# Placing loads on aligned runs of an on-chip arena, and asking for long loads at a smaller lead: a decode kernel bound by its loads

## The chip, the cores and the metric

The kernel runs on one core of one Trainium2 chip. The metric is device time in microseconds (us), median of several executions. Most kernels were timed in five rounds next to the kernel before, on the same chip. The spans of profiles (2343.0 us and so on) are those of one profiled execution. In the profiles PE is the matmul engine and PEld its weight loads, DVE, ACT and POOL are the vector, scalar and GpSimd engines, SP issues the loads; SBUF is the on-chip memory, in 128 partitions.

## The reference

Two layers of the same shape are applied twice to eight sequences with one new token each (`B = 8`, `D = 640`): attention over a cache, then a small feed-forward block.

```python
x = x + A(layernorm(x), k_cache, v_cache, wq, wo)   # layer 0
x = x + B(layernorm(x), w1, w2)
x = x + A(layernorm(x), k_cache, v_cache, wq, wo)   # layer 1, the same cache again
x = x + B(layernorm(x), w1, w2)
# A: q = x @ wq, 32 heads of 128; scores over 4096 cached keys, softmax, weighted sum of values, @ wo
# k_cache, v_cache: [8, 32, 4096, 128] bf16
```

One pass over both caches is 537 MB, and both layers need it, 1074 MB in all; the weights are 15 MB. There is one query per head, so there is little to compute per byte.

## The kernel before

All keys and values pass through one SBUF tile, the arena, of `G = 26` units. A unit is 4 KB in each of 128 partitions, 512 KB; one load is one DMA of `n` neighbouring units, from one run of memory to one run of the arena. For each batch entry layer 0 reads all its units in order; then comes the turn, and layer 1 reads them again. At the turn 21 units stay in the arena (`G - SPARE`) and three more are set aside, so that layer 1 need not load those 24 again. Over eight entries 1856 units are loaded out of 2048 read. While the 21 are kept, only five units are free, and loads are of one unit each.

A planner in Python decides, before anything runs, when each load is issued, how long it is and where it goes. It keeps a rough clock of the PE and of the loads; `lead` is how far the loads are planned to be ahead.

```python
G = 26
SPARE = 5
LEADS = ((9, 8), (6, 4), (5, 2))      # (lead in us, units): with that lead, a load has at least that many units
...
    def room(n):                      # where n free neighbouring units are; the longest free ones first
        us = [u for u in range(G - n + 1) if not any(owner[u : u + n])]
        return min(us, key=lambda u: max(freed[u : u + n])) if us else None

    def feed():                       # called whenever a unit has been read for the last time
        while at[0] < len(stream):
            lead = clock[1] - clock[0]
            calm = (PACE * (nth[stream[at[0]]] - at[1]) - LATE - lead) / 1.2
            least = next((n for us, n in LEADS if lead >= us), 1)
            least = min(least, max(1, (G - len(kept) - 2) // 3))
            most = min(max(least, int(calm)), LEADS[0][1], max(1, (len(stream) - at[0]) // 2))
            least = min(least, most)
            ...
            u = next((u for n in range(n, least - 1, -1) if (u := room(n)) is not None), None)
            if u is None:
                return                # no run of `least` units is free: hold out, issue nothing now
            ...
            ops.append(("load", b, p, n, u))
...
    def do_load(b, p, n, u):
        nc.sync.dma_start(out=arena[:, u * GW : (u + n) * GW], in_=A_kv[b, :, p * GW : (p + n) * GW])
```

A large lead makes the planner wait until a long run is free, in place of filling a short one at once.

## Time and profile before

| | before |
|---|---|
| median | 2340.99 us (6 runs, 2339.02 to 2343.42) |
| profiled span | 2343.0 us |
| moved by DMA | 990.87 MB |
| PE busy | 60% |
| rate between turns, most slices | 430 to 434 GB/s |

These are lines of the page of the kernel before: the span; the granted PE clock, the DMA share (tenths) and the rate in 40 slices of 58.6 us; two of the DMA queues with packets, megabytes and share of the 16 engines; the chain of waits by engine, then the head of its list by line.

```profile
span 2343.0 us, 43024 instructions
...
PEclk9999999999999998555555555555555555555555
DMA  9999999999999999999999999999999999999997
GB/s 411 430 433 401 433 432 432 431 396 432 432 432 430 404 434 431 430 427 403 433 432 431 426 412 434 430 432 420 427 431 427 432 416 430 431 431 431 396 433 329
...
q1 hardware_dynamic: 76564, 988.12, 99.4%
q8 instruction: 146, 2.39, 0.4%
...
DMA 71%; PE 17%; ACT 6%; DVE 3%; issue 2%; SPq 0%; POOL 0%; ACTq 0%; DVEq 0%; POOLq 0%
DMA arena<-in_A_kv_dram 71%; PE o_ps L687 5%; PE s_ps L695 4%; PE s_ps L705 2%; ACT P_row L755 2%; ACT o_sb L795 1%; PE small_ps L655 1%; DVE mrow L713 1%; ACT P_sb L761 1%; PE small_ps L800 1%; ACT arena L634 1%; PE small_ps L768 1%; PE small_ps L825 1%; DVE hmx L732 0%; ACT nmax L753 0%
```

The rate line is the one to read first. It stands mostly at 430 to 434 GB/s and dips at ten places: the first slice, the last one, and eight places about 280 us apart (401, 396, 404, 403, 412, 420, 416, 396) that hold the eight turns. The DMA share stays at 9 tenths through the dips: the engines are seldom idle there, they are less effective. The clock line falls to half at slice 17 and the rate line does not notice, so PE's speed is not what bounds this kernel. The Trainium skill's page "DMA: Bandwidth & Descriptors" (Specifications) gives 435 GB/s as the ceiling of the way into SBUF; the trace agrees, with 434 as the best slice. At 432.5 GB/s, 991 MB take 2291 us (worked out), so about 52 us of the span are open to any change of the loads.

These are lines of the page's list of DMA issues: count, KB of one, median us from issue to landing.

```profile
arena<-in_A_kv_dram SPq DMA_DIRECT2D x124, 4096.0 KB, 23.1
arena<-in_A_kv_dram SPq DMA_DIRECT2D x98, 2048.0 KB, 22.7
arena<-in_A_kv_dram SPq DMA_DIRECT2D x218, 512.0 KB, 6.5
arena<-in_A_kv_dram SPq DMA_DIRECT2D x48, 1024.0 KB, 11.3
```

The issue-to-landing time of 23 us for a 4096 KB load, whose bytes take 9.7 us, shows that such a load waits behind others. A one-unit load takes 6.5 us: at a turn it mostly has four others ahead of it (read from the issue and landing times), each 1.25 us.

### The profile page before, as it was taken

Reading aid. Unit: us, or ns where it says so; the run is one execution under the profiler, and the core shown is the slowest. Engines: PE = TensorE matmul, PEld = TensorE weight load, DVE = VectorE, ACT = ScalarE, POOL = GpSimd, SP = SyncE. Lnnn points to the kernel's source line nnn. Section 1 sums busy time; section 2 is a strip of 40 time slices with the busy share of each in tenths; the row PEclk is TensorE's granted clock in tenths of the full one; section 3 lists DMA queues with packets and bytes.
Section 4 is the critical chain, followed back from the end, with each engine's and each line's share of the span. In section 5 each row is a group of like instructions: output and inputs, shape, how many; then the busy total and the mean of one; then the engine's idle time right before and its main releaser. Section 6 shows DMA issues by size and latency. Waiting matters only on the chain.

```text
span 2343.0 us, 43024 instructions
## 1 busy us (share of the span) xinstructions
PE 1398.6 (60%) x18748; PEld 591.4 (25%) x18748; DVE 496.7 (21%) x2022; ACT 426.3 (18%) x986; POOL 59.5 (3%) x296
## 2 busy tenths in 40 slices
PE   3547654576545764557545675556755567545766
PEld 1214211152111511125111241113411133111523
DVE  1113211131112211122111221112211122111312
ACT  1111211122111221112211121111211112111211
POOL 0000000000000000000000000000000000000000
PEclk9999999999999998555555555555555555555555
DMA  9999999999999999999999999999999999999997
GB/s 411 430 433 401 433 432 432 431 396 432 432 432 430 404 434 431 430 427 403 433 432 431 426 412 434 430 432 420 427 431 427 432 416 430 431 431 431 396 433 329
DMA packets 76753, 990.87 MB, mean 423 GB/s; under 512 B 8596, under 2 KB 8596, under 8 KB 36500
## 3 DMA queue, kind: packets, MB, share of 16 engines
q1 hardware_dynamic: 76564, 988.12, 99.4%
q8 instruction: 146, 2.39, 0.4%
q14 instruction: 43, 0.35, 0.0%
HBM read 988.08 MB, written 0.01 MB: 422 GB/s over the span
## 4 chain that ended last, share of the span: by engine, by line
DMA 71%; PE 17%; ACT 6%; DVE 3%; issue 2%; SPq 0%; POOL 0%; ACTq 0%; DVEq 0%; POOLq 0%
DMA arena<-in_A_kv_dram 71%; PE o_ps L687 5%; PE s_ps L695 4%; PE s_ps L705 2%; ACT P_row L755 2%; ACT o_sb L795 1%; PE small_ps L655 1%; DVE mrow L713 1%; ACT P_sb L761 1%; PE small_ps L800 1%; ACT arena L634 1%; PE small_ps L768 1%; PE small_ps L825 1%; DVE hmx L732 0%; ACT nmax L753 0%
## 5 line engine op out<-in xcount | busy, mean ns | idle before, releaser
L687 PE MATMUL o_ps<-arena,P_sb 128*4 128x512 bf16 x3952 | 584.3, 596 | 402.0 <-DMA arena<-in_A_kv_dram 401.0
L695 PE MATMUL s_ps<-arena,qz 128*4 128x512 bf16 x3040 | 410.3, 602 | 261.1 <-DMA arena<-in_A_kv_dram 249.5
L687 PEld LDWEIGHTS <-P_sb 128*4 128x4 bf16 x3952 | 107.4, 88 | 502.8 <-issue 491.7
L713 DVE TENSOR_REDUCE mrow<-s_ps 100x1 bf16<-100x512 f32 x190 | 131.8, 694 | 323.2 <-PE s_ps L695 323.2
L795 ACT CAST o_sb<-o_ps 100x512 bf16<-100x512 f32 x247 | 144.9, 587 | 289.3 <-PE o_ps L687 286.0
L753 ACT ACTIVATE nmax<-small_ps 100x1 f32<-100x1 f32 x106 | 18.1, 171 | 774.5 <-PE small_ps L742 774.5
L775 DVE CAST P_sb<-small_ps 128x64 bf16<-128x64 f32 x190 | 42.6, 224 | 523.1 <-PE small_ps L768 523.1
L695 PEld LDWEIGHTS <-qz 128*4 128x4 bf16 x3040 | 63.9, 85 | 313.7 <-issue 295.5
L705 PEld LDWEIGHTS <-arena 128*128 128x128 bf16 x4224 | 129.6, 104 | 40.8 <-DMA arena<-in_A_kv_dram 23.4
L705 PE MATMUL s_ps<-qo,arena 128*128 128x1 bf16 x3712 | 123.7, 165 | 17.2 <-ACT P_sb L761 7.6
L768 PE MATMUL small_ps<-few,P_row 100*128 100x16 bf16 x760 | 52.3, 179 | 92.1 <-ACT P_row L755 92.1
L753 ACT ACTIVATE nmax<-small_ps,q_scale 100x1 f32<-100x1 f32 x84 | 22.0, 261 | 398.7 <-PE small_ps L742 398.7
L787 DVE TENSOR_REDUCE lsum<-small_ps 128x2 f32<-128x64 f32 x240 | 53.9, 224 | 171.9 <-PE small_ps L781 171.9
L768 PEld LDWEIGHTS <-P_row 100*128 100x128 bf16 x760 | 35.0, 107 | 186.5 <-ACT P_row L755 178.2
L720 PE MATMUL small_ps<-few,mrow 100*1 100x16 bf16 x190 | 34.4, 181 | 67.6 <-DVE mrow L713 67.6
L755 ACT ACTIVATE P_row<-s_ps,nmax 100x512 bf16<-100x512 f32 x106 | 72.8, 687 | 3.4
L800 PEld LDWEIGHTS <-o_sb 100*128 100x128 bf16 x988 | 45.7, 106 | 107.2 <-ACT o_sb L795 73.8
L655 PE MATMUL small_ps<-xq,wq_sb 128*128 128x1 bf16 x1200 | 48.8, 165 | 38.9 <-DVE qo L812 33.5
L800 PE MATMUL small_ps<-few,o_sb 100*128 100x2 bf16 x988 | 65.1, 170 | 10.7 <-DVE lsum L787 2.2
L727 DVE TENSOR_REDUCE diag<-small_ps 1x2 bf16<-1x16 f32 x190 | 30.8, 162 | 186.9 <-PE small_ps L720 186.9
L720 PEld LDWEIGHTS <-mrow 100*1 100x1 bf16 x190 | 15.0, 79 | 210.8 <-DVE mrow L713 210.8
L755 ACT ACTIVATE P_row<-s_ps,nmax,q_scale 100x512 bf16<-100x512 f32 x84 | 65.3, 778 | 2.8
(225 smaller groups left out, 958.0 us busy)
## 6 DMA issues: line engine op xcount, KB each, us to landing
arena<-in_A_kv_dram SPq DMA_DIRECT2D x124, 4096.0 KB, 23.1
arena<-in_A_kv_dram SPq DMA_DIRECT2D x98, 2048.0 KB, 22.7
arena<-in_A_kv_dram SPq DMA_DIRECT2D x218, 512.0 KB, 6.5
arena<-in_A_kv_dram SPq DMA_DIRECT2D x48, 1024.0 KB, 11.3
arena<-in_A_kv_dram SPq DMA_DIRECT2D x11, 3072.0 KB, 22.4
arena<-in_A_kv_dram SPq DMA_DIRECT2D x11, 2560.0 KB, 20.5
arena<-in_A_kv_dram SPq DMA_DIRECT2D x10, 1536.0 KB, 19.7
wq_sb<-in_A_wq_dram SPq DMA_DIRECT2D x4, 1280.0 KB, 17.6
```

The lines of the kernel that those rows point to most:

```text
L655: nc.tensor.matmul(q_ps[:, h : h + 1], lhsT=wq_sb[:, g, c, (2 * n + h) * Dh : (2 * n + h + 1) * Dh], rhs=xlns[b][:, 0, c : c + 1], start=( ...
L687: nc.tensor.matmul(o_ps[32 * c : 32 * c + CJ, :], lhsT=P_tiles[i][:, h, j : j + CJ], rhs=arena[:, at + c * CJ * Dh : at + (c + 1) * CJ * D ...
L695: nc.tensor.matmul(s_ps[32 * c : 32 * c + CJ, :], lhsT=qz[:, i % 3, c // 2, 3 - g : 3 - g + CJ], rhs=arena[:, at + c * BANK : at + (c + 1) ...
L705: nc.tensor.matmul(s_tiles[i][:, j : j + 1], lhsT=arena[:, at + n * P : at + (n + 1) * P], rhs=qo[:, b, h : h + 1], start=True, stop=True,)
L713: nc.vector.tensor_reduce(out=m_tiles[i][:OR, :1], in_=s_ps[:OR], axis=AX.X, op=ALU.max)
L720: nc.tensor.matmul(turn_ps[:1, : 4 * CJ], lhsT=m[:OR, :1], rhs=rsel[:OR], start=True, stop=True)
L755: nc.scalar.activation(out=P_rows[i][:OR], in_=s_ps[:OR], func=ACT.Exp, bias=nm[:OR, :1], scale=more)
L768: nc.tensor.matmul(P_ps[:, k * 4 * CJ : (k + 1) * 4 * CJ], lhsT=P_row[:OR, k * P : (k + 1) * P], rhs=rsel[:OR], start=True, stop=True,)
L775: nc.vector.tensor_copy(out=P_tiles[i].rearrange("p h (c k) -> p h c k", k=BANK // P), in_=P_ps.rearrange("p (k h c) -> p h c k", k=BANK / ...
L787: nc.vector.tensor_reduce(out=L, in_=(lsum2_ps if ahead[i] else lsum_ps).rearrange("p (h j) -> p h j", h=2), axis=AX.X, op=ALU.add)
L795: nc.scalar.copy(out=o_tiles[i][:OR], in_=o_ps[:OR, :].rearrange("p (j d) -> p j d", j=CJ))
L800: nc.tensor.matmul(oy[i][:, :2], lhsT=o_tiles[i][:OR, j, :], rhs=gsel[:OR, j, :], start=(j == 0), stop=(j == CJ - 1))
```

## The change

The intent: free runs on an 8-unit boundary (4-unit for shorter loads) are taken first, and loads of one or two units go into blocks already in use, so that whole blocks stay free for long loads. And a long load needs less lead than it did: with 7 us under way a load must have eight units (it took 9 us), with 5 us four (6), with 4 us two (5).

```diff
-LEADS = ((9, 8), (6, 4), (5, 2))
+LEADS = ((7, 8), (5, 4), (4, 2))
...
     def room(n):
         us = [u for u in range(G - n + 1) if not any(owner[u : u + n])]
-        return min(us, key=lambda u: max(freed[u : u + n])) if us else None
+        step = 8 if n > 4 else 4 if n > 2 else n
+
+        def cost(u):
+            block = owner[u // 8 * 8 : u // 8 * 8 + 8]
+            return u % step, -sum(block) if n <= 2 else 0, max(freed[u : u + n])
+
+        return min(us, key=cost) if us else None
```

The bytes, the order in which units are loaded and all compute work are the same. Only lengths, places and times of issue of the loads move.

## The prediction

> **What bounds the kernel now.** The loads of keys and values. The page's DMA part has 988 MB on queue 1, 430 to 434 GB/s in most of the 40 slices; PE is busy 60% and the chain of waits lies 71% in arena loads. The Trainium skill ("DMA: Bandwidth & Descriptors", Specifications) gives a ceiling of 435 GB/s; the trace agrees. At 432.5 GB/s all 991 MB would take 2291 us (my division), so only some 52 us of the 2343 us span can be won. Stretches of 5 us show where: 3 us at the start, 13.6 at the end (the last 10.6 have no load under way), and some 29 at eight turns from layer 0 to layer 1 of a batch entry, near 205, 490, 785, 1070, 1360, 1640, 1920 and 2190 us, 2.3 to 4.4 us each.
>
> **What goes on at a turn.** 21 of the 26 arena units hold kept data; the other five take loads of one unit (512 KB), three or four under way, landing every 1.25 us where long loads take 1.2125 us per unit, plus one to three single delays of 0.5 to 1.4 us. These come while loads are queued: the trace shows 16 KB packets on the instruction queue, each some 0.9 us, every 6 us at a turn and every 25 us elsewhere. Between turns the queue holds some 13 us of work at each issue, so no wait of the issuing queue costs anything there.
>
> **What the change does.** Bytes and compute work stay. Loads that the changed program issues: one-unit 218 to 207, two-unit 48 to 38, four-unit 98 to 63, eight-unit 124 to 149; 521 loads become 484. Eight-unit loads off an 8-unit boundary fall from 32 to 9. The five spare units at a turn, and so its one-unit loads, stay.
>
> **Cost.** A packet of 4 KB takes 167 ns on the mean against 152 at the long ones' rate, 8 KB 311 against 304, 16 KB 616 against 608. Fewer of them save, as an estimate, 11 x 128 x 15 ns / 16 = 1.3 us, 0.5 us and 2.4 us: 4.2 us at most. By landing times four-unit loads are no slower per byte when the queue is full, so I count 0.5 to 2 us. Perhaps 1 to 2 us more come from the first turn, the worst (about 5 us), whose pattern becomes like the others'. Holding out for long runs at a thinner lead may cost 1 us when the queue refills after a turn. In sum 2 to 4 us of 2341.
>
> **Prediction.** 2338 us, 2329 to 2346 in 8 of 10. Faster by over 2%: 1%; within 2%: 98%; slower: 1%.
>
> **What would show it.** Right: DMA issues with the counts above; eight dips of GB/s, still 2 to 4.5 us each; between turns 10 us or more queued at each issue; the last landing still 10 to 11 us before the end; 146 instruction packets. Wrong: dips half as deep (then fragmented short loads caused them), or new dips 20 to 60 us after each turn with PE waiting for the arena (then holding out drains the queue).
>
> **What would make it wrong.** A longer load waits for more units and lands all at once; if PE at the 0.5 clock of the second part falls behind there, DMA would starve. Or alignment itself speeds transfers in a way that landing times of before don't show. The last loads (5, 1, 2, 1, 1 units instead of 7, 4, 2, 1, 1) could move the end by a microsecond or two.

## The result, and the profile after

| | before | after |
|---|---|---|
| median | 2340.99 us (6 runs) | 2343.64 us (6 runs, 2341.00 to 2345.82) |
| ratio after over before | | 1.0011, 95% interval 0.9998 to 1.0024 |
| loads | 521 | 484 |

A ratio here and below is the mean time of one kernel's fast runs over the mean of the other's fast runs of the same rounds, so it is not quite the ratio of the medians quoted beside it. By this ratio the change is the same within noise; if anything it is slower.

The same lines of the page after:

```profile
span 2344.0 us, 42943 instructions
...
PEclk9999999999655555555555555555555555555555
DMA  9999999999999999999999999999999999999997
GB/s 411 431 431 402 431 431 432 431 410 434 430 434 428 405 429 430 431 428 404 435 431 431 423 410 432 432 432 417 415 434 433 430 413 422 431 432 430 395 433 337
...
q1 hardware_dynamic: 71236, 988.12, 99.4%
q8 instruction: 146, 2.39, 0.4%
```

```profile
arena<-in_A_kv_dram SPq DMA_DIRECT2D x149, 4096.0 KB, 23.0
arena<-in_A_kv_dram SPq DMA_DIRECT2D x63, 2048.0 KB, 13.8
arena<-in_A_kv_dram SPq DMA_DIRECT2D x207, 512.0 KB, 6.4
arena<-in_A_kv_dram SPq DMA_DIRECT2D x38, 1024.0 KB, 9.5
```

The counts are those forecast: 149 long loads in place of 124, 63 of four units in place of 98. The rate between turns is mostly 430 to 434 GB/s as before, and the eight dips are there (402, 410, 405, 404, 410, 415, 413, 395). Instruction packets are 146 in both. This chain of waits breaks off (its shares add up to 28% of the span), so it is not used. The granted clock of the six runs of the changed kernel lies between 0.62 and 0.94, and a higher clock did not go with a shorter time (2344.78 us at 0.94, 2341.00 at 0.62).

To see where the two differ, the landing times of loads were read from the two traces and set against the position in the stream of 1856 units, which is the same for both. About a quarter of the loads (129 of 521 before, 119 of 484 after) have no landing time in the profile's own view and were bridged by a straight line. Three sums over the run, each the time taken less 1.2125 us per unit, the pace of long loads:

- turn: from four units ahead of the first one-unit load of a turn to its last, 26 to 30 units, eight times (the bounds are those of the kernel before, and the same stretches of the stream are used for every kernel);
- refill: the 60 units after that, in which layer 1 gives the kept units free and the queue grows back, eight times;
- rest: all else after the first 160 units.

```
profiled kernel          turn  refill  rest   (us, sums over the run)
before                   25.0    6.9    9.8
after                    23.9   10.2    8.8
```

The missing landings can be got back: the records are short only because the load of `x` and the store of the result leave 11 of them where the other transfers leave 16. With every landing read, no sum in this text moves by more than 1.5 us (the two refills become 6.2 and 9.6).

So the turns lose about what they lost, and the refill loses 3 us more. That is the size of the whole difference, but single delays of about 1.2 us fall differently in every execution, so one pair of profiles does not prove it. Here is a refill in both: windows of 20 us after the seventh turn (busy us and count of instructions by engine, then clock, DMA share and rate). First the kernel before, with the header line:

```profile
core 0: us, PE busy (x) PEld busy (x) DVE busy (x) ACT busy (x) POOL busy (x), PEclk, DMA share, GB/s
1940.00:1960.00 20.00, 15.37 (x309) 9.31 (x307) 5.87 (x25) 8.80 (x21) 0.00 (x0) 0.50 1.02 425
1960.00:1980.00 20.00, 15.99 (x208) 6.14 (x209) 4.74 (x19) 5.42 (x14) 0.00 (x0) 0.50 1.02 434
1980.00:2000.00 20.00, 9.86 (x106) 3.27 (x99) 3.27 (x12) 3.42 (x7) 0.00 (x0) 0.50 1.00 428
```

Then the changed kernel:

```profile
1940.00:1960.00 20.00, 15.23 (x310) 9.25 (x308) 5.59 (x24) 8.56 (x21) 0.00 (x0) 0.50 1.02 423
1960.00:1980.00 20.00, 15.97 (x209) 6.27 (x207) 5.07 (x21) 5.50 (x14) 0.00 (x0) 0.50 1.01 420
1980.00:2000.00 20.00, 9.23 (x95) 2.74 (x94) 2.65 (x9) 3.00 (x7) 0.00 (x0) 0.50 1.00 431
```

In the middle window the changed kernel moves 420 GB/s where the kernel before moves 434. In the changed kernel's trace the loads issued there begin at 1952.0 and then at 1962.1 us, a gap of 10 us in which the planner (run again from its source) held out for seven or eight units and then for four; the kernel before issued at 1951.5, 1955.1 and 1961.5.

### The profile page after: what moved, and what is told of

Read it like the earlier page. It is cut to its first block, busy times and chain, and to the rows that moved or that the text cites. A ratio compares the mean times of both kernels' runs of the same rounds, so it can differ in the third digit from the quotient of the medians.

```text
span 2344.0 us, 42943 instructions
## 1 busy us (share of the span) xinstructions
PE 1392.3 (59%) x18748; PEld 591.7 (25%) x18748; DVE 496.6 (21%) x2022; ACT 426.3 (18%) x986; POOL 59.1 (3%) x296
## 5 line engine op out<-in xcount | busy, mean ns | idle before, releaser
L819 DVE TENSOR_TENSOR oT<-small_ps,invL 128x2 bf16<-128x2 f32 x120 | 19.1, 159 | 316.4 <-PE small_ps L807 315.4
```

## Experiments

Theory A: while loads are queued, their length and place cost next to nothing; the change can only act where the queue is short, and there its lower thresholds make the planner hold out for long runs when short ones would keep the queue fed. Rival B: the placement itself moves the time. Rival C: there is no difference at all.

### Each half alone

`align_only` has the new `room` with the old thresholds, `leads_only` the old `room` with the new thresholds:

```diff
 # align_only, against the changed kernel
-LEADS = ((7, 8), (5, 4), (4, 2))
+LEADS = ((9, 8), (6, 4), (5, 2))
 # leads_only, against the kernel before
-LEADS = ((9, 8), (6, 4), (5, 2))
+LEADS = ((7, 8), (5, 4), (4, 2))
```

> Only the placement rule of the change, old thresholds (9/8, 6/4, 5/2). Theory A (load shape costs nothing while loads are queued; what the change loses, it loses by holding out for long runs when the queue refills after a turn): within 1 us of before, 2340 to 2342 us, last landing near that of before (2332 us). Rival B (placement itself moves the time, through waits on more landings or through packets): all of the change's +2.6 us here, or a gain of 2 us or more. Rival C (the +2.6 us is noise): 2341 +- 1.5 us here and in the thresholds-only run.

> Only the thresholds of the change (7/8, 5/4, 4/2), old placement. Theory A: the whole loss is here, +2 to +3 us over before, with under 5 us of queued work at issues in the 40 us after a turn. Rival B: within 1 us of before. Rival C: within 1.5 us of before, no order between the two halves.

Measured: `align_only` 2339.68 us, ratio 0.9992 (0.9980 to 1.0005); `leads_only` 2343.90 us, ratio 1.0006 (0.9994 to 1.0019). Neither is clear of the kernel before. The order is the one that theory A asks for, but these two runs alone do not rule out C. They were repeated below.

### How much a load's length costs

`cap4` lets no load be over four units, `cap1` makes every load one unit:

```diff
-            most = min(max(least, int(calm)), LEADS[0][1], max(1, (len(stream) - at[0]) // 2))
+            most = min(max(least, int(calm)), 4, max(1, (len(stream) - at[0]) // 2))   # cap1: 1
```

> The kernel before with no load over four units: 380 four-unit loads in place of 98, and none of five to eight. Counting by packet times (616 ns for 16 KB against 608 at the long rate) this costs (380-98) x 128 x 8 ns / 16 = 18 us. Counting by landing times, with the queue full, 0 to 2 us. My theory is the second: 2340 to 2344 us. If the first is right, 2355 to 2360 us.

> The kernel before with one-unit loads only, 1856 of them. If a 512 KB load costs 1.25 us for its size alone (and not because only five units are free at a turn): 1638 more units x 0.0375 us = 61 us more, about 2400 us, landings every 1.25 us between turns too. If the 1.25 us belongs to the short queue at a turn: 1.2125 us between turns and a time within 10 us of before.

Measured: `cap4` 2344.66 us, ratio 1.0013 (1.0001 to 1.0026), 3 us and not 18, though just over the 2340 to 2344 that were expected. `cap1` 2397.43 us, ratio 1.0235 (1.0220 to 1.0251), 55 us. The rate and the issues of `cap4`:

```profile
GB/s 408 430 430 404 431 430 430 430 408 430 430 430 430 413 430 430 430 428 410 429 431 431 425 416 430 430 430 418 422 431 430 430 416 426 431 430 430 410 430 336
...
arena<-in_A_kv_dram SPq DMA_DIRECT2D x380, 2048.0 KB, 26.3
```

It moves 430 GB/s between turns, against 430 to 434 before. `cap1` in two windows between the first and the second turn:

```profile
300.00:340.00 40.00, 22.90 (x201) 7.83 (x199) 6.36 (x23) 7.00 (x15) 0.39 (x2) 0.50 1.03 418
340.00:380.00 40.00, 22.36 (x188) 7.75 (x187) 6.68 (x25) 5.95 (x12) 0.77 (x4) 0.50 1.03 419
```

and the kernel before in the same windows:

```profile
300.00:340.00 40.00, 20.89 (x210) 6.77 (x209) 6.53 (x24) 7.00 (x15) 0.39 (x2) 1.00 0.99 427
340.00:380.00 40.00, 21.07 (x199) 6.38 (x196) 7.30 (x28) 6.55 (x13) 0.77 (x4) 1.00 1.01 435
```

Here the loads of `cap1` have over 8 us of work ahead of them, no turn is near, and the rate is still 418 to 419 GB/s. So one unit costs 1.25 us by its own length (512 KB / 1.25 us = 419 GB/s), not because the queue is short. Four units in one load cure nearly all of it: they stay within 1% of the long rate. So the first half of theory A holds from four units up and not for one. A shorter load here also has shorter rows (4 KB in each partition for one unit, 16 KB for four), and no run varies the two apart. This is why 35 four-unit loads fewer had nothing to give, and it also says that the one-unit loads at the turns pay only 218 x 0.0375 = 8 us of the turns' loss for their length.

A packet's duration misled here, for two reasons. The mean of 616 ns for 16 KB, where the long rate would make 608, counts in 146 instruction packets of the same size, which take 933 ns each; the loads' own packets take 612 ns, and the same sum would then give some 10 us and not 18. And packets of one engine overlap (the DMA share above reads over 1), so that summing their excess still overstates the loss: 3 us on the clock.

### Holding out on purpose

`hold_out_more` is the changed kernel with thresholds lowered again:

```diff
-LEADS = ((7, 8), (5, 4), (4, 2))
+LEADS = ((2, 8), (2, 4), (1, 2))
```

> The changed kernel with thresholds lowered once more, (2, 8), (2, 4), (1, 2): it holds out for long runs with still less under way. Theory A (holding out at a thin lead loses time in the refill after a turn): 2 to 8 us slower than the changed kernel's 2343.6, so 2345 to 2352, with queued work of 2 to 3 us at issues for 40 us or more after a turn. Rival (thresholds don't matter, the 4 us between the two halves are noise): 2339 to 2343.

Measured: 2375.22 us, ratio 1.0141 (1.0125 to 1.0156), 33 us slower than the kernel before. The theory's sign is right, its size was far off. There are fewer loads than in the changed kernel (454 against 484, with 160 of eight units against 149), and yet the time is the worst of all kernels with mixed lengths. The windows after its seventh turn, which comes 25 us later here:

```profile
1965.00:1985.00 20.00, 15.46 (x330) 9.69 (x327) 5.70 (x24) 7.79 (x20) 0.00 (x0) 0.50 0.91 354
1985.00:2005.00 20.00, 12.68 (x182) 5.54 (x179) 3.65 (x16) 4.54 (x13) 0.00 (x0) 0.50 0.98 404
2005.00:2025.00 20.00, 10.86 (x108) 3.29 (x108) 3.26 (x12) 3.58 (x8) 0.00 (x0) 0.50 0.98 407
```

That is 354, 404 and 407 GB/s where the kernel before has 425, 434 and 428. The accounting by stream position puts the loss in one place: refill 37.6 us against 6.9, turn 26.7 against 25.0, rest 6.9 against 9.8. At three issues after this turn (at 1975.4, 1981.8 and 2013.1 us) the queue held 0.8, 0.7 and 2.6 us of work, against about 4 us or more at every issue in the same stretch of the kernel before. The last of the three is an eight-unit load that came 18 us after the issue ahead of it.

### The same question in the other direction, and the halves again

`after_again` and `align_again` are the changed kernel and its placement half once more, in the same rounds. `thresholds_up` is the placement half with higher thresholds:

```diff
-LEADS = ((9, 8), (6, 4), (5, 2))
+LEADS = ((10, 8), (7, 4), (6, 2))
```

> The changed kernel once more, beside its placement-only half in the same rounds. Theory A: 2 to 5 us over the placement-only half, with the refill after the turns (60 units each, less 1.2125 us per unit) losing about 10 us in sum, against about 7 in the kernel before. Rival C (all noise): no difference over 1.5 us.

> Placement rule alone once more. Theory A: 2338 to 2342 us, 0 to 2 us under the kernel before. Rival C: as the changed kernel.

> Placement rule with thresholds moved the other way, (10, 8), (7, 4), (6, 2): short loads go out for longer after a turn. If holding out is what costs, the refill loses 5 to 8 us in sum, and the time is 2337 to 2342 us, at or just under the placement-only half; more four-unit loads give some of it back. If thresholds only act through the number of loads (543), 2344 us or more.

Measured: `after_again` 2343.19 us (2341.12 to 2349.00), ratio 1.0013 (1.0000 to 1.0025); `align_again` 2339.47 us (2337.88 to 2340.56), ratio 0.9991 (0.9979 to 1.0004); `thresholds_up` 2341.78 us, ratio 1.0003 (0.9990 to 1.0015). All five runs of `align_again` are faster than all five of `after_again`, by 3.7 us between the medians and 5.0 between the means. Rival C falls: with the new placement, the thresholds alone cost 3 to 5 us. With the old placement (`leads_only`) they cost 1.5 us by the ratio, which is not clear of nothing. The refill follows the thresholds through all kernels with this or the old placement:

```
thresholds              kernel           turn  refill  rest   (us)
(10,8) (7,4) (6,2)      thresholds_up    28.5    3.5   10.9
(9,8)  (6,4) (5,2)      before           25.0    6.9    9.8
                        align_only       21.6    7.9    8.4
                        align_again      21.3    7.1    8.0
(7,8)  (5,4) (4,2)      after            23.9   10.2    8.8
                        after_again      20.5   11.9    9.6
                        leads_only       22.6    9.7    8.8
(2,8)  (2,4) (1,2)      hold_out_more    26.7   37.6    6.9
```

Two profiles of the same kernel differ by up to 3.4 us in a column, so only the order of the groups counts. It is without exception in the refill column, also for `misalign` below (8.6). `thresholds_up` has the smallest refill loss (3.5 us, under the 5 to 8 expected), but its profile shows more in the turn, and its time gains nothing: the optimum is flat, near where the thresholds already were.

### Alignment turned round

`misalign` is the changed kernel with the first part of the key reversed, so that runs off the boundary are preferred; 68 eight-unit loads then start off an 8-unit boundary, against 9 in the changed kernel and 32 before:

```diff
-            return u % step, -sum(block) if n <= 2 else 0, max(freed[u : u + n])
+            return u % step == 0, -sum(block) if n <= 2 else 0, max(freed[u : u + n])
```

> The changed kernel with the placement turned round: a free run off the boundary is preferred (68 eight-unit loads start off an 8-unit boundary, against 9). If alignment has no worth of its own: within 2 us of the changed kernel, 2342 to 2346. If alignment itself speeds loads or their issue: over 2347 us.

Measured: 2344.33 us, ratio 1.0014 (1.0000 to 1.0027), beside 2343.19 us for the changed kernel in the same rounds. Alignment has no worth of its own that these runs could show. That the placement half came out at 0.9992 and 0.9991 may be a gain of 2 us, but each interval includes 1, and no run shows by what it would come.

### What the rest of a turn's loss is: three tries, not settled

Length explains about 1 us of each turn's three or so. Two suspects were tried: the short queue, and the instruction packets, which are closer together at a turn.

`spare8` keeps three units fewer per entry, so that eight are free at a turn (`SPARE = 8`, kernel before otherwise).

> The kernel before with eight spare units at a turn in place of five (three fewer kept per batch entry): 24 more units loaded, 29.1 us of transfer at 1.2125 us. If the turn's delays come from the short queue (three or four units under way), a longer queue takes back about half of the turns' 29 us: 2352 to 2360 us in all. If they don't depend on the queue's length, 2370 us.

Measured: 2364.02 us, ratio 1.0098 (1.0085 to 1.0112), 23 us more for 29 us of added transfer. So about 6 us come back, less than the half that was expected. Both stated outcomes missed. The run does not show that the longer queue gave them: it also has 94 one-unit loads in place of 218, and 124 x 0.0375 = 4.7 us would come from their length alone.

`fetch_turn` and `fetch_between` add memsets of one unused element on POOL, which bring more instruction packets, near the turns or away from them:

```diff
     def do_mm(which, i, g, u):
+        near = any(t - 4 <= i < t + 5 for t in turned_to)      # turned_to: first visits of layer 1
+        for _ in range(8 if near else 0):                       # fetch_between: 8 if not near
+            nc.gpsimd.memset(few.bitcast(BF16)[:, 3:4], 0.0)
```

> The kernel before with 8 memsets of one element on POOL (otherwise idle) per arena unit near a turn, over 4000 in all, about 32 more instruction packets of 8 KB. Theory F (the single delays at a turn are instruction packets that hold up one DMA engine while the queue is short): +6 to +15 us. Rival (the delays have another cause): within 2 us of before. If POOL's own work at the turn is held up, PE will be seen to wait for POOL, and the run settles nothing.

> The same memsets away from the turns, over 11000, some 90 more packets of 8 KB while the queue holds 10 us or more. Theory F: a packet costs its share of 16 engines only, 90 x 0.309 / 16 = 1.7 us, at most twice that: 2342 to 2345 us. Rival (every instruction packet holds up the loads by 0.3 us or more wherever it falls): +27 us or more.

The queues of instruction packets, in `fetch_turn` and then in `fetch_between`; before, the second line read 43 packets:

```profile
q8 instruction: 146, 2.39, 0.4%
q14 instruction: 79, 0.65, 0.1%
```

```profile
q8 instruction: 146, 2.39, 0.4%
q14 instruction: 135, 1.11, 0.1%
```

Measured: `fetch_turn` 2342.95 us, ratio 1.0005 (0.9993 to 1.0018); `fetch_between` 2371.74 us, ratio 1.0130 (1.0116 to 1.0144). This is the opposite of what theory F asked for, but the two runs settle less than it seems. PE waited for POOL's memsets in both, first `fetch_turn`, then `fetch_between` (us in total, times, longest), and no such wait is in the kernel before:

```profile
PE s_ps L700 <- POOL few L679: 15.4, 6, 3.5
```

```profile
PE s_ps L700 <- POOL few L679: 65.6, 23, 5.8
```

The first expectation had said that a run with such waits settles nothing. And of the 36 more packets of `fetch_turn` only 11 fell into the turn stretches (18 into the refills): at 0.3 us each they would cost 3 us, which the interval does not exclude. Theory F is neither shown nor refuted. In `fetch_between` the loss lies between the turns (rest 31.9 us against 9.8; turn 24.0, refill 10.3), where 10 us or more stayed queued at every issue, so PE's waits did not drain the queue. 92 more packets came with 30 us there, 0.33 us each, about what one such packet takes in the trace (0.309 us). The rival of `fetch_between`, that every packet holds up the loads wherever it falls, met its number but not the other run, where 36 packets would make 11 us. The Trainium skill ("DMA: Bandwidth & Descriptors", Queues, rings and completion order) says that each DMA engine goes round its queue rows packet by packet. That fits packets that delay loads on their engine. If POOL's packets all use one engine, and that engine has some slack against the others, both runs would fit; the traces do not name the engine of a packet, so this is only a guess. The memsets themselves may also play a part.

The kept traces hold one more answer. The memsets added packets of 8 KB on queue 14, but the prediction had meant those of 16 KB on queue 8 (0.93 us each, 146 in each run), whose number no run changed; 45 of the 146 fall into the turn stretches, 317 us of the 2343. Every landing of a one-unit load that follows another one-unit load (after the first 180 us) was set against the packets that began between 1 us before the landing ahead of it and 1.25 us after. How late these landings come, against a step of 1.25 us:

```
traces            16 KB packet near      only an 8 KB packet      neither
before            0.20 us (55)           0.02 us (6)              0.03 us (136)
13, without cap1  0.15 us (755)          0.02 us (107)            0.02 us (1514)
cap1              0.10 us (229)          0.02 us (85)             0.00 us (1421)
```

So the 16 KB packets go with some 9 us of the loss in the kernel before (55 x 0.17), and the 8 KB packets that the two runs added go with nothing at a turn. In `cap4` alone the difference is small (0.06 against 0.04 us). This is a coincidence in time over many landings, not an experiment. What makes the single delays at a turn stays open.

## Why the prediction was right, and where it was off

- **The time: inside the range, on the wrong side of before.** 2338 us (2329 to 2346) against 2343.64. "Same" at 98% was right. A saving of 2 to 4 us was argued; the measured change is about 2.6 us the other way, and its interval just includes none. That 2343.64 still lies inside is owed to the width of the range, 17 us, and not to the account of the gain: that the number fell inside in spite of the wrong sign was luck.
- **What bounds the kernel: right.** Rate, dips and share are as read. Runs at granted clocks from 0.56 to 1.00 (`cap1`, 2394.34 to 2400.28 us) take the same time within 6 us, and the kernel before took 2341.61 us at 1.00 and 2342.11 at 0.57 in one set of rounds, which rules PE's speed out.
- **Counts, between-turn rate and instruction packets: right**, as the lines after show. The last landing came 10.2 us before the end, as forecast. The eight dips stayed: 25.0 us of turn loss in the profile before, 23.9 and 20.5 in two profiles after.
- **"I count 0.5 to 2 us" for fewer short packets: right in kind.** The landing view was the right one and the packet view wrong: `cap4` lost 3 us and not 18. The placement half came out 2 us faster, twice, each time within its interval.
- **"Perhaps 1 to 2 us more come from the first turn": failed.** The first turn lost 4.5 us before, 3.8 and 4.8 in two profiles after. Making its pattern like the others' gave nothing that can be seen.
- **"Holding out for long runs at a thinner lead may cost 1 us": the step that turned the sign.** The mechanism was right and the size was off: refill 10.2 and 11.9 us against 6.9, so 3 to 5 us, and 3.7 us between the medians of `after_again` and `align_again`. The prediction gives no working for its 1 us; `hold_out_more` shows how fast this loss grows when the thresholds go down further, 31 us more in the refill.
- **The instruction packets as the cause of the single delays: open.** They were given as a cause from their coincidence alone. The coincidence holds over all kept traces together (0.15 us late against 0.02); the tests with POOL's packets added packets of another size on another queue, so they say nothing against it.
- **"If PE at the 0.5 clock of the second part falls behind, DMA would starve": did not happen** between turns. Some 13 us stayed queued in most of the run. "10 us or more queued at each issue" was missed at six issues clear of the turns and refills, and the shallowest of them, 6.8 us ahead, still lost nothing.

Where did the expected gain go? Most of it was never there: with the queue full, four units in one load are all but as good as eight. The rest was given back in the refill. The best version seen is the placement half alone, 2339.47 and 2339.68 us, which beats the changed kernel clearly and the kernel before only by an amount within noise.

## What to carry to other kernels

Make loads long only up to the point where the landing pace stops improving, and measure that pace from landings with a full queue, not from the sum of packet durations; here it was reached at or before four units (2 MB), and one unit (512 KB) cost 3%. Where the queue is short, a short load now is worth more than a long one later: for a rule that waits for a long free run, a smaller lead cost 3 to 5 us here, and a larger one gained nothing. When a change moves both where things go and how long it waits, time the two halves in the same rounds, since they may have opposite signs.

## What the Trainium skill lacked or had wrong

- "DMA: Bandwidth & Descriptors", Rules for kernel authors, advises 1 MiB or more per DMA for bandwidth. The page's table of rates by size is of loads issued from GpSimd, and it has none for loads from SyncE that queue behind one another: here 512 KB loads of 4 KB rows land every 1.25 us (419 GB/s) with over 8 us queued, against 430 GB/s with 2 MB loads and 430 to 434 with mixed longer ones. The advice agrees with these runs, and it is worth at most 3% of the rate here.
- The same page, in its closing note on tile shapes, leaves open whether few large or many small descriptors are faster. Loads of one unit, with rows of 4 KB, reached 97% of the rate of long loads with rows of 32 KB here; the length of the load and of its rows changed together.
- The same page names the row that carries runtime-internal traffic, but no page has a figure for what instruction packets cost a kernel bound by loads. One-unit landings with a 16 KB packet near came 0.15 us late on the mean, others 0.02. 92 more packets of 8 KB came with 30 us in one run; 36 more came with nothing clear in another.
- No page warns that packet durations of one engine add up to more than the time, so that the DMA share reads over 1 (1.03 in two windows of `cap1`, at 418 and 419 GB/s) while the rate is down.
